# A planner that may put copies, roundings, lines and half of a weight's shift on either of two engines, and that reckons with instruction fetches

## The chip, the core and the metric

The kernel runs on one core of a Trainium2 chip. The metric is the device time of one execution in microseconds. The core has a matrix engine (PE), three engines for elementwise work (DVE, the vector engine; ACT, the scalar engine; POOL, GpSimd), and a queue on SP from which all loads and stores are issued to 16 DMA engines. Each engine takes its instructions strictly in order: an instruction that waits holds up all behind it on its engine.

## The reference

Attention over keys and values that are pooled eight to one, then a feed-forward layer whose activation is a rational function.

```python
k_p = k.reshape(B, H, Sp, pool, D).mean(axis=3)      # q, k, v: (8, 8, 576, 64), pool = 8
v_p = v.reshape(B, H, Sp, pool, D).mean(axis=3)
scores = scale * np.matmul(q, k_p.transpose(0, 1, 3, 2))
scores = scores - np.max(scores, axis=-1, keepdims=True)
attn = np.exp(scores)
attn = attn / (np.sum(attn, axis=-1, keepdims=True) + 1e-09)
x = np.matmul(attn, v_p)                              # as (4608, 512)
h = x @ w_in                                          # w_in: (512, 2048), w_out: (2048, 512)
P = a[0] + a[1] * h + a[2] * h2 + a[3] * h3           # h2 = h * h, h3 = h2 * h
Q = 1.0 + np.abs(b[0]) * np.abs(h) + np.abs(b[1]) * h2
out = (P / (Q + 1e-6)) @ w_out                        # the weights and a, b come as float64
```

## The kernel before

The 4608 tokens are 18 blocks of 256. The 2048 hidden columns are 8 units of 256, each with one slice of `w_in` and one of `w_out`. A step is one unit of one block in the first eight steps (blocks 0 and 1, units 0 to 3), later one half unit of two blocks. Its work is `mm1` (PE, into a PSUM bank `ph`), `rational` (tiles `w`, `r`, `rp`, `t`, then `gh` and `gl`, the rounded part and the rest) and `mm2` (PE, sums in two banks `po` of each block). Matrix products are made of float32 operands split in a rounded part and a rest, three products each. Blocks get their `x` by attention: `q` is loaded, turned by PE (`pq`) and copied by ACT (`qT`), PE makes `ps`, DVE, ACT and POOL the softmax `e`, PE turns that (`pm`, copies `am`) and makes `pv`, from which ACT and DVE split `x`. From block 4 on turning is done by DVE and small DMAs (`am<-e`, `am<-er`). The first eight steps, with four blocks of attention, eight weight slices and most large loads, fill the first 95 us or so; it is called the start here.

A float64 weight slice (`load_weights`) is turned to float32 thus: ACT makes `m` from the high words; for each half of the columns DVE shifts `m` left by three bits into a bank (`sh`) and joins to it the three top bits of the low word; ACT rounds the result into the weight and POOL makes the rest. In `quotient` (one rational), ACT makes `w` and `t` from `ph` and `r` from `w`, POOL multiplies `w` by `r`, DVE works on `t`, ACT makes `rp` (log, exp), DVE three more products, ACT rounds `gh`, and POOL makes `gl`.

The order on each engine is set by `Plan.solve`, a list scheduler that runs when the program is built. Every operation is tied to one engine, has a cost and a due time; the planner takes the operation that can start first, and among those within a window (`WIN`) the one of the lowest due time plus `SLOPE` times its delay. DMAs are costed by one bus that is free from `FIRST` on, and a landing time. `issue` writes the instructions out in that order (line 358 in the profile); where the plan leaves PE free while a `po` sum is open, it puts in small matmuls that add zeros to that sum, and before the first steps matmuls into a bank `idle` (line 349 both). They are called fillers here.

## Time and profile before

| | us |
|---|---|
| median of 3 runs (lowest to highest) | 871.18 (869.35 to 871.55) |
| the profiled execution | 871.99 |
| its span, from the first instruction to the last | 870.2 |
| PE busy | 853.6 (98%) |
| DVE busy | 684.1 (79%) |
| ACT busy | 637.6 (73%) |
| POOL busy | 566.1 (65%) |

The span is a little shorter than the execution's time; the rest lies around it. Fillers count as busy PE time. A group of instructions in the profile is named by output and inputs, without buffer numbers, so `gh<-t` is the rounding of all steps. In the timeline, the figure in brackets is how long the engine sat idle before the instruction and what ended that.

### The profile page before, as it was taken

The numbers are of one execution on the slowest core, as the hardware profiler recorded it, in microseconds if no ns is written. First come the engines' busy times: TensorE is split into PE (matmuls) and PEld (weight loads), VectorE is DVE, ScalarE is ACT, GpSimd is POOL, SyncE is SP. The second block draws the span as 40 slices with busy tenths as digits, with TensorE's granted clock in tenths as the row PEclk, the third lists the DMA queues.
The fourth block names the chain that finished last, engine by engine and source line by source line (L and its number), as shares of the span: only waits on it lengthen the run. The fifth ranks groups of instructions, "written<-read, shape, count | busy, mean of one in ns | idle before, by whom it ended". The sixth has DMA issues, their size and how long they took to land.

```text
span 870.2 us, 16357 instructions
## 1 busy us (share of the span) xinstructions
PE 853.6 (98%) x5628; PEld 745.9 (86%) x5628; DVE 684.1 (79%) x1155; ACT 637.6 (73%) x1098; POOL 566.1 (65%) x548
## 2 busy tenths in 40 slices
PE   8989999999999999999999999999999999999998
PEld 7779888898788888888888888878888888888897
DVE  5888998977877888868786878777877787876664
ACT  4889799875767776768777676868676777776764
POOL 4977788985767664677556765767666646464543
PEclk9999999999999999999999999999999999999999
DMA  9995621126244222224224422253124222020001
GB/s 323 324 336 171 193 48 49 32 57 171 62 95 92 74 34 51 42 71 92 68 32 89 99 40 54 65 106 67 38 43 102 38 54 32 30 35 27 25 1 50
DMA packets 191031, 74.23 MB, mean 85 GB/s; under 512 B 162276, under 2 KB 171876, under 8 KB 190948
## 3 DMA queue, kind: packets, MB, share of 16 engines
q1 hardware_dynamic: 190948, 73.18, 33.2%
q8 instruction: 45, 0.74, 0.4%
q14 instruction: 38, 0.31, 0.1%
HBM read 49.41 MB, written 12.58 MB: 71 GB/s over the span
## 4 chain that ended last, share of the span: by engine, by line
PE 81%; DMA 6%; SPq 4%; POOL 3%; issue 2%; ACT 2%; DVE 2%; POOLq 0%; DVEq 0%
PE po L358 37%; PE ph L358 37%; SPq L358 4%; DMA q<-in_q_dram 4%; PE pv L358 2%; PE ps L358 2%; POOL gl L358 1%; DVE t L358 1%; DMA early<-in_v_dram 1%; DMA st_k<-in_k_dram 1%; PE pm L358 1%; DMA st_r<-st_r 1%; PE po L349 1%; DMA ob<-pd 0%; POOL st_k L358 0%
## 5 line engine op out<-in xcount | busy, mean ns | idle before, releaser
L358 PE MATMUL ph<-x,win 128*128 128x512 f32 (+1 forms) x1920 | 428.1, 360 | 1.9 <-DVE t L358 0.7
L358 PEld LDWEIGHTS ph<-x,win 128*128 128x128 f32 x1920 | 337.2, 189 | 45.0 <-issue 2.1
L358 PE MATMUL po<-wout,gh 128*128 128x512 f32 x1152 | 288.9, 383 | 2.6 <-ACT gh L358 1.3
L358 POOL TENSOR_TENSOR w<-w,r 128x512 f32<-128x512 f32 (+1 forms) x145 | 184.8, 1275 | 115.6 <-ACT r L358 101.0
L358 POOL TENSOR_TENSOR gl<-t,gh 128x512 fp32r<-128x512 f32 (+1 forms) x145 | 184.4, 1273 | 95.5 <-ACT gh L358 87.3
L358 PEld LDWEIGHTS po<-wout,gh 128*128 128x128 f32 x1152 | 223.1, 198 | 26.6 <-ACT rp L358 1.5
L358 DVE SCALAR_TENSOR_TENSOR t<-t,abn,rp 128x512 f32<-128x512 f32 (+1 forms) x145 | 106.8, 737 | 98.1 <-ACT rp L358 97.4
L358 PE MATMUL po<-wout,gl 128*128 128x512 f32 x576 | 156.5, 381 | 0.0
L358 ACT ACTIVATE rp<-w 128x512 f32<-128x512 f32 (+1 forms) x145 | 86.9, 600 | 62.8 <-POOL w L358 53.4
L358 ACT ACTIVATE w<-ph 128x512 f32<-128x512 f32 (+1 forms) x145 | 85.9, 592 | 63.3 <-PE ph L358 59.2
L358 PEld LDWEIGHTS po<-wout,gl 128*128 128x128 f32 x576 | 112.4, 198 | 11.5
L358 ACT ACTIVATE t<-ph,abn 128x512 f32<-128x512 f32 (+1 forms) x145 | 111.1, 769 | 11.3 <-PE ph L358 11.1
L358 ACT ACTIVATE r<-w,abn 128x512 f32<-128x512 f32 (+1 forms) x145 | 116.9, 806 | 1.3 <-DVE rp L358 0.7
L358 DVE TENSOR_TENSOR t<-t,ph 128x512 f32<-128x512 f32 (+1 forms) x145 | 98.4, 678 | 22.7 <-ACT t L358 17.0
L358 DVE SCALAR_TENSOR_TENSOR t<-t,abn,ph 128x512 f32<-128x512 f32 (+1 forms) x145 | 106.6, 735 | 1.9 <-ACT w L358 0.2
L358 ACT CAST gh<-t 128x512 fp32r<-128x512 f32 (+1 forms) x145 | 88.8, 613 | 23.2 <-DVE t L358 21.2
L358 DVE SCALAR_TENSOR_TENSOR t<-rp,t 128x512 f32<-128x512 f32 (+1 forms) x145 | 98.3, 678 | 1.4
L358 DVE SCALAR_TENSOR_TENSOR rp<-w,rp 128x512 f32<-128x512 f32 (+1 forms) x145 | 99.0, 683 | 0.3
L358 ACT ACTIVATE rp<-rp 128x512 f32<-128x512 f32 (+1 forms) x145 | 84.8, 585 | 1.5
L358 POOL TENSOR_TENSOR e<-e,sm 128x576 f32<-128x576 f32 x36 | 40.9, 1151 | 7.6 <-DVE sm L358 6.3
L358 POOL TENSOR_TENSOR st_v<-st_v 128x512 f32<-128x512 f32 (+1 forms) x28 | 28.2, 1007 | 25.8 <-DMA st_v<-in_v_dram 24.6
L358 POOL TENSOR_TENSOR st_k<-st_k 128x512 f32<-128x512 f32 (+3 forms) x36 | 31.3, 868 | 19.3 <-DMA st_k<-in_k_dram 18.3
(99 smaller groups left out, 654.5 us busy)
## 6 DMA issues: line engine op xcount, KB each, us to landing
out_dram<-ob SPq DMA_DIRECT2D x17, 512.0 KB
rwin<-in_moe_w_in_dram SPq DMA_DIRECT2D x8, 1024.0 KB
rwout<-in_moe_w_out_dram SPq DMA_DIRECT2D x8, 1024.0 KB
st_v<-in_v_dram SPq DMA_DIRECT2D x28, 256.0 KB
am<-e SPq DMA_DIRECT2D x224, 32.0 KB
st_k<-in_k_dram SPq DMA_DIRECT2D x12, 512.0 KB
q<-in_q_dram SPq DMA_DIRECT2D x144, 32.0 KB
am<-er SPq DMA_DIRECT2D x224, 16.0 KB
```

The costliest lines, as they stand in the source:

```text
L349: self.nc.tensor.matmul(to, lhsT=self.filler, rhs=one, start=first, stop=first, skip_group_check=True)
L358: getattr(engines[op.eng], name)(*map(value, args), **{k: value(v) for k, v in kw.items()})
```

## The change

Operations can now have several ways, one per engine, each with its own cost (`Either`), and `solve` takes the engine on which such an operation can start first, after a handicap (`YIELD`) for the engine that is not its own. Copies and evictions (`copy`) may go to ACT or DVE, roundings (`cast`: `gh`, the weight, `kr`, `er`, `kpT`) to ACT or POOL, the line `t` to ACT or DVE, the line `r` to ACT or POOL. The left shift may be replaced: ACT then takes the top 16 bits of the low word and makes its three top bits by a scale and a rounding (bias `floor`), and DVE's joining instruction does the shift of `m` itself.

The planner also counts PE's instructions (two for each matmul and its weight load, four for those of unrounded float32), expects an instruction fetch at every 249 of them, and lets it delay DMAs that are under way by 1.15 us. Some costs and the windows have new values.

Over the whole program the order moves 84 of 143 full `r` and 47 of 143 `gh` from ACT to POOL, 35 of 143 full `t` from ACT to DVE, ten of 18 `ob` evictions on DVE to ACT, two `wout` and one `win` rounding and all seven `kr` to POOL; 15 of 32 shifts become an ACT instruction. In the start these are three `r`, five `gh` and one `wout` rounding on POOL, three `t` on DVE, and eight of the sixteen shifts of the first eight weight slices on ACT. Fillers: 50 into `idle` where 56 were; 48 into `po` in the first steps where 37 were, 39 of them in one place; and 7 later where one was.

```diff
@@ -151,13 +157,16 @@
     SURE = 20.0
 
     LOOK = 0.02
-    WIN = {"sp": 0.02, "pe": 0.02, "pool": 0.8, "dve": 0.02, "act": 0.3}
-    SLOPE = 20.0
+    WIN = {"sp": 0.02, "pe": 0.02, "pool": 0.3, "dve": 0.02, "act": 0.3}
+    SLOPE = 80.0
 
     SPARE, AFTER, SAFE = 0.0, 1.0, 0.0
 
     DEPTH = 128
-    FIRST, FLY, LAND = 3.1, 0.65, 0.6
+    FIRST, FLY, LAND = 2.35, 0.65, 0.6
+    FETCH, LONG, STEP = 249, 1.15, 0.108
+
+    YIELD = {"dve": 0.8, "act": 0.0, "pool": 0.0}
 
     MOVED = {}
 
...
@@ -237,8 +252,8 @@
             for e, cands in engs.items():
                 opts = found[e] = []
                 for op in cands:
-                    t = max(at[e], op.ready)
-                    if op.port:
+                    t = max(at[e], op.ready[e] + (self.YIELD[e] + op.shy if e != op.eng else 0.0))
+                    if op.ways[e][2]:
                         t = max(t, port)
                     if op.bytes:
                         t = max(t, landed[-8])
@@ -271,11 +286,14 @@
                 t, op = min(((t, op) for t, op in opts if t <= t0 + self.WIN[e]),
                             key=lambda x: (x[1].due + self.SLOPE * (x[0] - t0), x[1].seq))
                 if best is None or t < best[0]:
-                    best = t, op
+                    best = t, op, e
             assert best, "the plan is stuck at " + ", ".join(
                 str([b.name for b in op.bufs]) for c in engs.values() for op in c[:3])
-            t, op = best
-            engs[op.eng].remove(op)
+            t, op, e = best
+            for x in op.ways:
+                engs[x].remove(op)
+            op.eng = e
+            op.cost, op.calls, op.port = op.ways[e]
             for b in op.bufs:
                 if not b.held:
                     b.held = True
@@ -290,6 +308,19 @@
                 b.by[op.eng] = op.done
             if op.port:
                 port = op.end
+            if op.eng == "pe":
+                if t > at["pe"] and t < 100:
+                    steps += 2 * int((t - at["pe"]) / (0.215 if t < self.WARM else 0.12))
+                steps += op.steps
+                if steps >= goal:
+                    fetched = max(t, op.end - (steps - goal) * self.STEP / 2)
+                    goal += self.FETCH
+                    bus = max(bus, fetched) + self.LONG
+            if op.eng == "sp":
+                coming = max(at["pe"], t) + (goal - steps) * self.STEP
+                for x in (fetched, coming):
+                    if t < x + self.LONG and x < op.end:
+                        op.end = max(op.end, x + self.LONG + 0.4)
             if op.bytes:
                 begin = max(bus, op.end + self.FLY)
                 bus = begin + op.bytes
@@ -300,7 +331,9 @@
                 first, some, since, took = flow[oldest]
                 if issued - self.DEPTH > first:
                     op.end = max(op.end, since + took * (issued - self.DEPTH - first) / some)
-                op.done = bus + self.LAND + min(1.2, 0.4 * op.bytes) + (self.SAFE if bus > 100 else 0.0)
+                op.done = bus + self.LAND + min(0.4, 0.4 * op.bytes) + (self.SAFE if bus > 100 else 0.0)
+                if coming < op.done:
+                    op.done += self.LONG
                 landed.append(op.done)
             at[op.eng] = op.end
             for b in op.bufs:
...
@@ -372,6 +407,21 @@
                     self.eng, cost, [(name, args, kw)], port or self.eng == "pool", claims,
                     after=after)
         return Call()
+
+
+class Either:
+
+
+    def __init__(self, *ways):
+        self.ways = ways
+
+    def __call__(self, *args, claims=()):
+        (engine, n, name, extra), *others = self.ways
+        op = getattr(engine(n, claims=claims), name)(*args, **extra)
+        for engine, n, name, extra in others:
+            op.ways[engine.eng] = (engine.fixed + n * engine.rate / 1000, [(name, args, extra)],
+                                   engine.eng == "pool")
+        return op
 
 
 @with_exitstack
@@ -440,6 +490,17 @@
     dve = Engine(plan, "dve", 0.1, 1.04)
     act = Engine(plan, "act", 0.105, 0.85)
     gp = Engine(plan, "pool", 0.242, 2.021)
+    gp1 = Engine(plan, "pool", 0.2, 0.82)
+
+    def copy(n, first=act, scale=None):
+        ways = [(act, n, "copy", {}), (dve, n, "tensor_copy", {})]
+        if scale is not None:
+            ways = [(act, n, "activation", dict(func=AF.Copy, scale=scale)),
+                    (dve, n, "tensor_scalar", dict(scalar1=scale, scalar2=None, op0=ALU.mult))]
+        return Either(*ways) if first is act else Either(*ways[::-1])
+
+    def cast(n):
+        return Either((act, n, "copy", {}), (gp1, n, "tensor_copy", {}))
 
     def pe(ns, calls, claims=(), after=()):
         return plan.add("pe", ns / 1000, calls, claims=claims, after=after)
...
@@ -529,17 +592,23 @@
         hw, lw = words[:, :, 1], words[:, :, 0]
         m = new("dec", "m", [P, CW], F32, f"m_{name}")
         mi = m.bitcast(I32)
-        act(CW + 100).activation(m, hw.bitcast(F32), AF.Prelu, scale=2.0 ** -111, alpha=-2.0 ** 32)
+        act(CW + 250).activation(m, hw.bitcast(F32), AF.Prelu, scale=2.0 ** -111, alpha=-2.0 ** 32)
         for h in range(2):
             at = slice(h * CW // 2, (h + 1) * CW // 2)
             bits = bank(f"sh_{name}_{h}", [P, CW // 2]).bitcast(I32)
-            dve(CW // 2).tensor_scalar(
+            n = CW // 2
+            top = raw.bitcast(U16).rearrange("p (n t) -> p n t", t=4)[:, at, 1]
+            moved = dve(n).tensor_scalar(
                 out=bits, in0=mi[:, at], scalar1=3, scalar2=None, op0=ALU.logical_shift_left)
-            dve(CW // 2).scalar_tensor_tensor(
-                out=mi[:, at], in0=lw[:, at], scalar=29, in1=bits, op0=ALU.logical_shift_right,
-                op1=ALU.bitwise_or)
+            moved.ways["act"] = (act.fixed + (n + 130) * act.rate / 1000, [(
+                "activation", (bits, top, AF.Identity), dict(bias=floor, scale=2.0 ** -13))], False)
+            made = dict(out=mi[:, at], op1=ALU.bitwise_or, in1=bits)
+            low = dict(made, in0=lw[:, at], scalar=29, op0=ALU.logical_shift_right)
+            high = dict(made, in0=mi[:, at], scalar=3, op0=ALU.logical_shift_left)
+            both = dve(n).scalar_tensor_tensor(**low)
+            both.follow = moved, {"dve": both.calls, "act": [("scalar_tensor_tensor", (), high)]}
         w = new(kind, name, [P, 2, CW], F32R, name)
-        act(CW).copy(w[:, 0, :], m)
+        cast(CW)(w[:, 0, :], m)
         gp(CW).tensor_tensor(out=w[:, 1, :], in0=m, in1=w[:, 0, :].bitcast(F32),
                              op=ALU.subtract)
         weights[kind, u] = w
...
@@ -857,10 +922,7 @@
         pm = bank(name, [P, 4, P])[:SP]
         pe(110 * 4, [("transpose", (pm[:, x, :], row, ident), {}) for x, row in enumerate(rows)],
            claims=(am,))
-        if c == 0:
-            act(4 * P).copy(to, pm)
-        else:
-            dve(4 * P).tensor_copy(to, pm)
+        copy(4 * P, dve if c else act)(to, pm)
 
     def half(i, c, am, qs, es):
 
...
@@ -1088,8 +1150,12 @@
 
     def quotient(W, h, t, w, r, rp, gh, gl, early, late):
         act(W, claims=early).activation(w, h, AF.Abs, scale=1.0 / WS)
-        act(W + 200).activation(t, h, AF.Identity, bias=na2, scale=na3)
-        act(W + 260).activation(r, w, AF.Identity, bias=b0, scale=b1)
+        Either((act, W + 200, "activation", dict(func=AF.Identity, bias=na2, scale=na3)),
+               (dve, W + 100, "tensor_scalar", dict(scalar1=na3, scalar2=na2, op0=ALU.mult,
+                                              op1=ALU.add)))(t, h)
+        Either((act, W + 260, "activation", dict(func=AF.Identity, bias=b0, scale=b1)),
+               (gp1, W + 110, "tensor_scalar", dict(scalar1=b1, scalar2=b0, op0=ALU.mult,
+                                                   op1=ALU.add)))(r, w)
         gp(W).tensor_tensor(out=w, in0=w, in1=r, op=ALU.mult)
         dve(W).tensor_tensor(out=t, in0=t, in1=h, op=ALU.mult)
         dve(W + 50).scalar_tensor_tensor(
@@ -1102,7 +1168,7 @@
             out=rp, in0=w, scalar=QC, in1=rp, op0=ALU.add, op1=ALU.mult)
         dve(W).scalar_tensor_tensor(
             out=t, in0=rp, scalar=-2.0, in1=t, op0=ALU.add, op1=ALU.mult)
-        act(W, claims=late).copy(gh, t)
+        cast(W)(gh, t, claims=late)
         gp(W).tensor_tensor(out=gl, in0=t, in1=gh.bitcast(F32), op=ALU.subtract)
 
     pos, parts = {}, {}
@@ -1173,10 +1239,7 @@
 
     def evict(m, dst, po):
         dst, po = halves(dst), sorted_out(po)
-        if m == 0:
-            dve(DM).tensor_scalar(out=dst, in0=po, scalar1=1.0 / WS, scalar2=None, op0=ALU.mult)
-        else:
-            act(DM).activation(dst, po, AF.Copy, scale=1.0 / WS)
+        copy(DM, act if m else dve, 1.0 / WS)(dst, po)
 
 
     steps = [((i,), u, None) for i, u in
```

The order shows the move at three places. In the names the block or tile number stands behind the letters, then the unit; `pq6` turns the queries of tile 6, the first half of block 3.

**PE in the start**, where the sums of block 0 begin; `gh0_0` is the rounded rational of block 0 and unit 0. Before:

```order
L358 MATMUL ph0_3_839<-x_97,win3_796 128x256 x4
L358 MATMUL ph1_2_913<-x_97,win2_579 128x256 x16
L358 MATMUL po0_0_0_945<-wout0_693,gh0_0_747 128x512
L358 MATMUL po0_0_1_947<-wout0_693,gh0_0_747 128x512
L358 MATMUL pq6_950<-identr_95,q3_790 128x128 x4
L358 MATMUL po0_0_0_945<-wout0_693,gh0_0_747 128x512
```

And now:

```order
L393 MATMUL po0_0_0_939<-wout1_860,gl0_1_955 128x512
L393 MATMUL po0_0_1_941<-wout1_860,gl0_1_955 128x512
L393 MATMUL pq6_1036<-identr_95,q3_829 128x128 x4
L384 MATMUL po0_0_1_941<-zero_96,identr_95 128x256
L393 MATMUL ph1_3_1046<-x_97,win3_775 128x256 x24
L384 MATMUL po0_0_1_941<-zero_96,identr_95 128x256 x39
L393 MATMUL po0_0_0_939<-wout2_1041,gh0_2_1098 128x512
L393 MATMUL po0_0_1_941<-wout2_1041,gh0_2_1098 128x512
```

`pq6` stood behind the first two of block 0's `po` products; it now stands behind 24 of them (all of units 0 and 1), and eight more `ph1_2` products and four groups of `pm` stand ahead of it too. The wait for `gh0_2`, to which no filler led before, now has 39 ahead of it. On ACT the copy of `pq6` into `qT` moves with it from row 72 to row 84; on SP one of two stores of block 1's `x` (512 KB) has moved behind the load of `q3`.

**ACT in the first 20 us**, where the first two weights are made (`m_win0`, `m_win1`) and the softmax of block 0 is finished (`sm0`, `am0`). Before:

```order
L358 ACTIVATE sm0_0_282<-sm0_0_282,tiny_99 128x8
L358 COPY vp0_287<-pvs0_0_268 72x256
L358 ACTIVATE e0_238<-e0_238 128x576
L358 ACTIVATE m_win1_334<-rwin1_189 128x1024
L358 ACTIVATE sm0_1_301<-sm0_1_301,tiny_99 128x8
L358 COPY am0_0_347<-pm0_0_0_321 72x512
L358 COPY am0_0_347<-pm0_0_1_326 72x512
L358 CAST win0_356<-m_win0_279 128x1024
```

And now:

```order
L393 ACTIVATE sm0_0_277<-sm0_0_277,tiny_99 128x8
L393 ACTIVATE sh_win0_0_284<-rwin0_145,floor_100 128x512
L393 ACTIVATE sh_win0_1_287<-rwin0_145,floor_100 128x512
L393 ACTIVATE e0_234<-e0_234 128x576
L393 COPY vp0_295<-pvs0_0_264 72x256
L393 CAST win0_300<-m_win0_275 128x1024
L393 ACTIVATE sm0_1_297<-sm0_1_297,tiny_99 128x8
L393 COPY am0_0_344<-pm0_0_0_321 72x512
L393 COPY am0_0_344<-pm0_0_1_326 72x512
L393 ACTIVATE m_win1_348<-rwin1_185 128x1024
```

The second weight's first step stood ahead of the second sum `sm0_1` and both copies `am0_0`; now it stands behind them, and the two shifts and the rounding of the first weight stand ahead of them instead.

**POOL near the end of block 0's units 4 to 7**, some 205 us into the span before (`st_k3` are loaded keys of batch 3, `st_v2` loaded values of batch 2). Before:

```order
L358 TENSOR_TENSOR w0_6_2579<-w0_6_2579,r0_6_2591 128x512
L358 TENSOR_TENSOR gl0_5_2676<-t0_5_2471,gh0_5_2665 128x512
L358 TENSOR_TENSOR st_k3_0_2597<-st_k3_0_2597 128x2x256
L358 TENSOR_TENSOR w0_7_2626<-w0_7_2626,r0_7_2691 128x512
L358 TENSOR_TENSOR st_k3_0_2597<-st_k3_0_2597 128x2x128
L358 TENSOR_TENSOR ks3_0_2732<-st_k3_0_2597 128x256
L358 TENSOR_TENSOR gl0_6_2745<-t0_6_2550,gh0_6_2738 128x512
L358 TENSOR_TENSOR gl0_7_2789<-t0_7_2656,gh0_7_2778 128x512
```

And now:

```order
L393 TENSOR_TENSOR gl0_5_2605<-t0_5_2445,gh0_5_2579 128x512
L393 TENSOR_SCALAR r0_7_2625<-w0_7_2615,abn_449 128x512
L393 TENSOR_TENSOR st_v2_1_2572<-st_v2_1_2572 128x2x256
L393 TENSOR_TENSOR st_v2_1_2572<-st_v2_1_2572 128x2x128
L393 TENSOR_TENSOR vp0_295<-st_v2_1_2572 128x128
L393 TENSOR_TENSOR w0_7_2615<-w0_7_2615,r0_7_2625 128x512
L393 TENSOR_TENSOR gl0_6_2686<-t0_6_2519,gh0_6_2654 128x512
L393 TENSOR_TENSOR st_k3_0_2664<-st_k3_0_2664 128x2x256
L393 TENSOR_TENSOR gl0_7_2791<-t0_7_2621,gh0_7_2782 128x512
```

The first sum of `st_k3` stood ahead of `w0_7` and `gl0_6`; it now stands behind both, the sums of `st_v2_1` stand ahead of `w0_7` in its place, and `r0_7` is now POOL's too.

## Rows read from the trace of the kernel before

**Rows 1.** Windows view; columns: stretch, length, PE, PEld, DVE, ACT, POOL, clock, DMA, GB/s:

```profile
28.00:57.50 29.50, 28.25 (x341) 25.65 (x332) 28.90 (x59) 26.96 (x48) 27.73 (x25) 1.00 1.04 345
57.50:62.60 5.10, 1.73 (x9) 1.36 (x9) 4.99 (x9) 1.03 (x1) 3.40 (x3) 0.83 0.80 191
62.60:96.50 33.90, 33.90 (x321) 29.80 (x319) 28.41 (x51) 29.09 (x49) 24.61 (x21) 0.98 0.52 163
...
200.00:257.00 57.00, 54.01 (x349) 45.27 (x348) 45.15 (x78) 38.09 (x70) 40.37 (x42) 1.00 0.44 106
257.00:866.30 609.30, 608.11 (x3759) 530.42 (x3758) 469.71 (x783) 437.52 (x766) 369.73 (x353) 1.00 0.26 56
```

**Rows 2.** Timeline of PE (start, length, what; in brackets its idle before):

```profile
25.30 0.66 PE L358 MATMUL pq<-identr,q 128*128 128x128 f32 x4 [0.53 <-DMA q<-in_q_dram]
...
61.51 1.09 PE L358 MATMUL pq<-identr,q 128*128 128x128 f32 x4 [3.37 <-DMA q<-in_q_dram]
...
210.35 1.14 PE L358 MATMUL po<-wout,gh 128*128 128x512 f32 x4 [1.29 <-ACT gh L358]
...
227.55 1.06 PE L358 MATMUL po<-wout,gh 128*128 128x512 f32 x2 [1.16 <-DVE ob L358]
```

**Rows 3.** Windows view around 61 us, the same columns:

```profile
60.50:61.00 0.50, 0.00 (x0) 0.00 (x0) 0.50 (x2) 0.00 (x0) 0.40 (x1) 0.84 0.08 18
61.50:63.00 1.50, 1.49 (x6) 1.41 (x7) 0.99 (x2) 0.36 (x1) 0.00 (x0) 0.50 0.81 258
63.00:64.00 1.00, 1.00 (x4) 0.82 (x3) 0.00 (x0) 0.91 (x3) 0.00 (x0) 0.50 1.04 406
64.00:65.00 1.00, 1.00 (x5) 0.85 (x5) 0.05 (x1) 1.00 (x3) 0.00 (x0) 0.87 1.10 436
```

**Rows 4.** DMA view, 52.0 to 52.5 us: instruction queue (packets, MB, share):

```profile
q8 instruction: 1, 0.02, 12.3%
```

**Rows 5.** Timeline of ACT and DVE, first work after PE's wait:

```profile
62.64 0.58 ACT L358 COPY qT<-pq 128x512 f32<-128x512 f32 x1 [4.11 <-PE pq L358]
...
64.95 0.75 DVE L358 SCALAR_TENSOR_TENSOR t<-t,abn,rp 128x512 f32<-128x512 f32 x1 [2.46 <-ACT rp L358]
```

**Rows 6.** Timeline of ACT, of POOL, and the chain of work (115.75):

```profile
55.99 0.61 ACT L358 CAST gh<-t 128x512 fp32r<-128x512 f32 x1
...
58.52 1.28 POOL L358 TENSOR_TENSOR gl<-t,gh 128x512 fp32r<-128x512 f32 x1
...
115.75 1.73 PE po L358 x8
```

**Rows 7.** Timeline of PE, fillers in front of a pv product:

```profile
79.12 1.36 PE L349 MATMUL po<-zero,identr 128*128 128x256 f32 x10
```

**Rows 8.** Groups by shape, whole run (xcount | busy us, mean ns | idle before):

```profile
L358 POOL TENSOR_TENSOR w<-w,r 128x512 f32<-128x512 f32 x143 | 183.4, 1282 | 114.0 <-ACT r L358 99.4 <-DVE t L358 9.3 <-DMA q<-in_q_dram 3.5
...
L358 ACT ACTIVATE r<-w,abn 128x512 f32<-128x512 f32 x143 | 115.8, 809 | 1.3 <-DVE rp L358 0.7
...
L358 ACT CAST gh<-t 128x512 fp32r<-128x512 f32 x143 | 88.0, 616 | 21.2 <-DVE t L358 19.2 <-PE po L358 0.9 <-PE pk L358 0.4
...
L358 DVE TENSOR_SCALAR sh_win<-m_win 128x512 int32<-128x512 int32 x16 | 10.7, 694 | 3.7 <-ACT m_win L358 3.7
...
L358 ACT ACTIVATE m_win<-rwin 128x1024 f32<-128x1024 f32 x8 | 10.3, 1288 | 2.6 <-DMA rwin<-in_moe_w_in_dram 2.6
...
L358 POOL MEMSET pairs<- 128x208 f32 x1 | 0.3, 271 | 0.0
```

**Rows 9.** Timeline of ACT, the second weight's first step:

```profile
18.52 1.13 ACT L358 ACTIVATE m_win<-rwin 128x1024 f32<-128x1024 f32 x1 [2.62 <-DMA rwin<-in_moe_w_in_dram]
```

**Rows 10.** Timeline of POOL, and its waits (us, times, longest us):

```profile
206.03 1.27 POOL L358 TENSOR_TENSOR st_k<-st_k 128x512 f32<-128x512 f32 x1 [3.86 <-DMA st_k<-in_k_dram]
...
POOL st_v L358 <- DMA st_v<-in_v_dram: 24.6, 11, 5.9
...
POOL st_k L358 <- DMA st_k<-in_k_dram: 18.3, 10, 3.9
```

80 lines of the change are left out of this document (45 added, 35 removed).

## The prediction

> **What bounds the kernel now.** I read the page's busy times first. PE is busy for 853.6 of 870.2 us, so the other engines matter only where PE waits for them. The windows view then says where that is. From 257 us to PE's end PE is busy for 608.11 of 609.30 us; in the start and in the passage from 200 to 257 us, where it has 54.01 of 57, it is not [rows 1]. From 28 to 57.5 us DVE is busy for 28.90 of 29.50 us, more than any other engine: there it is the fullest. The timeline of PE names the waits: 3.37 us for a `q` load at 61.51, 0.53 us for another at 25.30, 1.29 us for `gh` at 210.35 and 1.16 us for `ob` at 227.55 [rows 2]. Two losses hide in the busy time: fillers, and 61.5 to 65 us, where the granted clock is 0.50 and then 0.87 behind the long wait [rows 3]. Of PE's two levels, 1.2 and 2.4 GHz, 0.50 is the lower.
>
> The long wait is the reader's main exhibit. PE stands in front of `pq`, behind it in order the `po` products. ACT has the copy of `pq` next and idles 4.11 us, DVE behind ACT 2.46 us [rows 5]. One late load stops three engines. While PE waits the DMA engines move 18 GB/s at a busy share of 0.08 [rows 3], about one engine of 16: all but one have brought their part. Eight us earlier an instruction fetch took 12.3% of 16 engines for 0.5 us [rows 4], that is 0.125 x 16 x 0.5 = 1.0 us of one engine. That the late engine is the one with the fetch is a reading; the rows don't name engines.
>
> The page "Runtime: NRT & Kernel Launch" of the Trainium skill (Instruction fetch mechanics) speaks against reckoning with fetches: the sequencer streams its code by itself, and the cost of crossing a block is mostly hidden. It holds for the engine that fetches; the row shows 1.0 us that the loads beside it don't get. By that rule the first rival below would have no chance; by the row it keeps its own.
>
> **The change, part by part.** The sum is made against the profiled execution, 871.99 us with a span of 870.2, and carried over to the median, 871.18, which is 0.8 lower.
>
> *The wait at 61.51.* `pq6` now has 22 more `po` products ahead of it. Eight take 1.73 us [rows 6], 0.216 each, so 22 take 4.8 us; eight `ph` products and four groups of `pm` come on top and aren't counted. PE came to the wait at 61.51 - 3.37 = 58.14, and would now come at 62.9 or later; the load had landed by 61.5. Cover of 1.4 us, and one store of 512 KB has left its front. Do the products' inputs hide it? `gh` of unit 1 ended at 55.99 + 0.61 = 56.60 and `gl` at 58.52 + 1.28 = 59.80 [rows 6], while the first `gl0_1` product comes 16 products, 3.5 us, after 57.5, at 61.0. They do. ACT's copy now stands 12 rows later, at 0.6 us or more each 7 us, against its 4.11 us of idling. The 3.37 us go, and with them the slow clock: half of 2.5 us and 0.13 of 1 us, 1.38. **-4.75**; ends -4.75 and, if the load is late again, -1.4.
>
> *Fillers.* Ten take 1.36 us [rows 7], 0.136 each. In the first steps 11 more: **+1.5**. Next late after the removed wait is `gh0_2`, and the 39 fillers there, 5.3 us, stand whether it is ready or not; so PE can't come out ahead of them. Six more later: +0.8, counted with the passage. Six fewer in `idle` are put at 0, since loads end the waits there.
>
> *Engines in the start.* Eight shifts leave DVE at 0.694 us [rows 8], -5.6; three `t` come at about the same price, +2.1; net -3.5 of the 28.9 us in which it is full. ACT gets eight shifts at half the price of a 1024-column step from the same raw weight, 1.288 / 2 = 0.64, +5.2, and loses three `r` (0.809) and five `gh` (0.616), -5.5: even. POOL gets eight of these and a `wout` rounding. The trace has no copy or line on POOL. Its nearest rows are a memset of 208 columns, 0.271 us, and a two-input product of 512 columns, 1.282 us [rows 8]. I take the memset scaled to 512 columns, 0.67, as one input is nearer to none than to two loops of the same; ends 0.27 and 1.28. That makes 8 x 0.67 + 1.33 = 6.7 us, and POOL has 33.90 - 24.61 = 9.3 us free from 62.6 to 96.5 [rows 1]: covered; at 1.28 it is 12.6 and isn't. PE loses 29.50 - 28.25 = 1.25 us from 28 to 57.5, of which a freer DVE can give back 0 to 1.25: **-0.6**.
>
> The page "GPSIMD Engine Reference" of the Trainium skill (When to use GPSIMD, Engine selection) speaks against POOL for elementwise work, but says that one-input work runs roughly at line rate; its 1.03 cycles an element at 1.2 GHz give an estimate of 0.44 us and a start-up for 512 columns. No row here shows it. By that the third rival has less chance than by rows alone.
>
> *First 28 us.* ACT's wait of 2.62 us for a weight load at 18.52 [rows 9] no longer stands ahead of `sm0_1` and `am0_0`; but two shifts and a rounding do, which wait for DVE. What PE gains is mostly lost again in front of the `q` load at 25.30 [rows 2], except for products done meanwhile: eight `ph` of half a `po`'s columns, 0.9 us. **-0.4**, ends -0.9 and +0.5.
>
> *The passage from 200 to 257 us.* POOL waited 3.86 us for `st_k` [rows 10] with `w` and `gl` behind it, and PE's 1.29 us at 210.35 followed. Both now stand ahead of that load: -1.3. In its place stand sums of `st_v2`, a load issued earlier. The 1.16 us for `ob` wait on a load and stay. With the six fillers **-0.5**; ends -2.2 (all 2.99 us lost there go, fillers stay) and +1.3 (POOL is caught by the other load).
>
> *From 257 us on.* PE waits 1.19 us in all. ACT, DVE and POOL have room: POOL gets 131 operations, 88 us at 0.67, on 566.1, and comes to 654 of 870 (75%); at 1.28 to 734 (84%). **0**, ends -1.2 and the third rival.
>
> Sum: -4.75 + 1.5 - 0.6 - 0.4 - 0.5 = -4.75; 871.99 becomes 867.2, and the median 871.18 becomes 866.4.
>
> **The rivals.** *The load is late again.* The plan's moments for fetches differ from the chip's, and a fetch or the stores meet `q3` anew; cover is 1.4 us. ACT then holds `rp0_2` behind the copy, DVE the next step of `t`, and `gh0_2` comes after its 39 fillers. For it speaks that a single engine's lateness cost over 1 us [rows 3]; against it, the extra work ahead. The first term keeps its 1.38 only: 866.4 + 3.4 = 869.8.
>
> *All waits go.* Fuller use of DVE and ACT and later `st_k` sums clear what can be cleared: lower ends throughout, -4.75 + 1.5 - 1.25 - 0.9 - 2.2 - 1.2 = -8.8, 862.4. Against it: the fillers show that waits remain in the plan.
>
> *POOL becomes the bound, and the kernel slower.* One-input work costs 1.28 us. From the first moved `r` of block 1 on, six such operations follow on POOL in the start; each is 0.61 longer, 3.7 us in front of `gh` and `gl`, if POOL has no slack. Later it is 84% busy, and its waits for loads, 11 for `st_v` and 10 for `st_k` [rows 10], of which I can follow one to PE, are not made up: four more that cost 1.29 us each are 5.2. 866.4 + 8.9 = 875.3. It decides from some 1.0 us an operation on (half of that excess takes the gain). For it: POOL's own rows are slow; against it: it waits 114.0 us in front of `w` alone [rows 8], so it has slack in most steps.
>
> **How the numbers follow.** The forecast, 864 to 868.5, has 0.58; all waits go 0.15; the load late again 0.17; POOL the bound 0.10. About 0.3%, 2.6 us, is what a measurement of this kernel can tell from no change, so faster means under 868.6 and slower over 873.8. Forecast and clear-out make 0.73, less 0.04 for the forecast's upper edge: faster 0.69. Late load and that edge make 0.21, and 0.01 of POOL's case: same 0.22. Slower 0.09. The range runs from 862.0, the clear-out, to 871.0, past the late load; POOL's case and the tails, some 0.15, are outside.
>
> **What would show it.** Right: no wait over 0.5 us on PE and a granted clock of 1.00 from 50 to 70 us; a block of 39 fillers with little idle time behind it; one-input POOL rows near 0.67 us; the wait at 210 gone; the passage's PE loss nearer to 1.5 than to 3 us. Wrong: PE idle behind the fillers at `gh0_2` by more than 2 us; a `q` load that ends a wait over 2 us in the start; POOL one-input rows over 1.0 us; more than 3 us of PE idle after 257 us, which would mean that the new order is worse where I put 0.

## The result, and the profile after

| | median, us | lowest to highest | runs |
|---|---|---|---|
| before | 870.26 | 868.57 to 871.55 | 4 |
| changed | 858.58 | 858.41 to 858.70 | 4 |

The ratio is 0.9867 (95% interval 0.9847 to 0.9887): 11.7 us faster, where 4.8 were forecast. The time lies below the range (862.0), and so below the 862.4 of the rival in which all waits go.

The page of the changed kernel, busy times:

```profile
PE 848.6 (99%) x5639; PEld 744.5 (87%) x5639; DVE 690.1 (81%) x1155; ACT 549.0 (64%) x954; POOL 662.2 (77%) x693
```

Windows view, the stretches of [rows 1] (columns as there):

```profile
28.00:57.50 29.50, 29.42 (x359) 27.42 (x351) 28.45 (x56) 27.91 (x49) 29.36 (x26) 1.00 1.07 344
57.50:62.60 5.10, 5.10 (x34) 4.53 (x33) 4.55 (x9) 5.03 (x8) 5.10 (x6) 1.00 0.95 273
62.60:96.50 33.90, 33.90 (x289) 29.49 (x288) 28.56 (x52) 28.13 (x45) 30.11 (x26) 1.00 0.60 194
...
200.00:257.00 57.00, 57.00 (x357) 49.51 (x350) 45.39 (x76) 34.76 (x65) 47.55 (x53) 1.00 0.39 92
257.00:853.00 596.00, 596.00 (x3710) 520.84 (x3708) 476.48 (x789) 350.11 (x627) 441.73 (x464) 1.00 0.26 55
```

From 28 us to its end PE has 0.08 us of gaps. Waits view of PE, all that it lists; every one lies before 27 us:

```profile
PE idle L393 <- DVE identr L1316: 1.8, 1, 1.8
PE pk L393 <- DVE early L393: 0.9, 2, 0.7
PE pm L393 <- POOL e L393: 0.8, 1, 0.8
PE pq L393 <- DMA q<-in_q_dram: 0.7, 2, 0.5
```

ACT fell from 637.6 to 549.0 us and POOL rose from 566.1 to 662.2. The groups by shape of what was moved, and of the product `w` behind POOL's `r` (columns as in [rows 8]):

```profile
L393 POOL TENSOR_TENSOR w<-w,r 128x512 f32<-128x512 f32 x143 | 183.5, 1283 | 15.6 <-ACT r L393 11.3
...
L393 POOL TENSOR_SCALAR r<-w,abn 128x512 f32<-128x512 f32 x84 | 64.9, 773 | 75.2 <-ACT w L393 71.6 <-DMA q<-in_q_dram 1.0 <-PE po L393 0.8
...
L393 POOL CAST gh<-t 128x512 fp32r<-128x512 f32 x47 | 28.8, 613 | 13.0 <-DVE t L393 11.6 <-PE ph L393 0.9 <-POOL ks L393 0.2
```

```profile
L393 ACT ACTIVATE sh_win<-rwin,floor 128x512 int32<-128x512 uint16 x8 | 6.5, 844 | 0.0
```

```profile
L393 DVE TENSOR_SCALAR t<-ph,abn 128x512 f32<-128x512 f32 x35 | 28.1, 804 | 14.4 <-ACT w L393 11.8 <-POOL st_r L393 1.4 <-POOL gh L393 0.8
```

POOL makes an `r` in 0.773 us and a `gh` in 0.613; DVE's `t` takes 0.804 and ACT's shift 0.844. ACT's shift takes longer than the one on DVE that it replaces (0.694 [rows 8]). POOL's wait in front of `w` went from 114.0 us [rows 8] to 15.6, but 75.2 us now stand in front of the `r` that it makes itself.

**A measure for all that follows.** Idle time understates what PE loses. A wait costs some 0.2 to 0.3 us more than its gap until products follow each other at full pace again: in the kernel before, by the measure below, the gap of 0.66 us in front of the `ph` at 30.34 costs 0.89, and the 1.29 us at 210.35 cost 1.62. This is called a restart here. And a fall of the clock hides in busy time. So I summed every trace thus. The distance from each matmul's start to the next start, less the median distance for its shape and tile over all traces, is loss, and so is the time up to PE's first instruction; a filler counts with its whole distance, and apart. The products alone come to 792.7 us in every trace, and products, fillers and loss make PE's end.

| us | products | fillers | other loss | PE's end |
|---|---|---|---|---|
| before, first trace | 792.7 | 16.6 | 57.4 | 866.7 |
| before, second trace (e9) | 792.7 | 16.0 | 55.8 | 864.5 |
| changed, first trace | 792.7 | 16.7 | 43.7 | 853.1 |
| changed, second trace (e13) | 792.7 | 16.8 | 44.3 | 853.9 |

Each row is one execution, the profiled one. Most of the loss seems to belong to the program (changes of shape, runs of small products): no kernel here came below 43.7. So the fillers cost in sum what they cost before, and the whole gain is loss that went: waits, the restarts behind them and slow clock.

The long wait, in the timeline of PE of the changed kernel and, of POOL, the `gh0_2` for which the 39 fillers stand:

```profile
62.30 0.60 PE L393 MATMUL pq<-identr,q 128*128 128x128 f32 x4
...
65.53 4.53 PE L384 MATMUL po<-zero,identr 128*128 128x256 f32 x39
69.90 0.60 PE L393 MATMUL po<-wout,gh 128*128 128x512 f32 x2
```

```profile
68.13 0.61 POOL L393 CAST gh<-t 128x512 fp32r<-128x512 f32 x1
```

`pq6` comes at 62.30 with no wait, and the clock of 1.00 stays. `gh0_2` is done at 68.74; its first product starts 1.16 us after that, behind the fillers.

### The profile page after: what moved, and what is told of

It reads as the page before. It is cut to its first block, busy times and chain, and to the rows that moved or that the text cites. A ratio compares the mean times of both kernels' runs of the same rounds, so it can differ in the third digit from the quotient of the medians.

```text
span 856.6 us, 16346 instructions
## 1 busy us (share of the span) xinstructions
PE 848.6 (99%) x5639; PEld 744.5 (87%) x5639; DVE 690.1 (81%) x1155; ACT 549.0 (64%) x954; POOL 662.2 (77%) x693
## 4 chain that ended last, share of the span: by engine, by line
PE 97%; DMA 2%; ACT 0%; SPq 0%; DVE 0%; issue 0%
PE po L393 44%; PE ph L393 44%; PE pv L393 3%; PE ps L393 3%; DMA q<-in_q_dram 1%; PE po L384 1%; DMA early<-in_k_dram 1%; PE pm L393 1%; PE pk L393 1%; PE pq L393 0%; SPq L393 0%; PE pvs L393 0%; DVE early L393 0%; PE pl L393 0%; PE pw L393 0%; ACT kpT L393 0%
## 5 line engine op out<-in xcount | busy, mean ns | idle before, releaser
L393 PE MATMUL ph<-x,win 128*128 128x512 f32 (+1 forms) x1920 | 418.8, 360 | 0.0
L393 POOL TENSOR_TENSOR w<-w,r 128x512 f32<-128x512 f32 (+1 forms) x145 | 185.0, 1276 | 15.6 <-ACT r L393 11.3
L393 POOL TENSOR_SCALAR r<-w,abn 128x512 f32<-128x512 f32 (+1 forms) x85 | 65.5, 770 | 75.8 <-ACT w L393 72.2
L393 ACT ACTIVATE t<-ph,abn 128x512 f32<-128x512 f32 (+1 forms) x109 | 84.1, 773 | 26.6 <-PE ph L393 24.2
L393 ACT CAST gh<-t 128x512 fp32r<-128x512 f32 (+1 forms) x98 | 59.9, 612 | 36.8 <-DVE t L393 34.4
L393 ACT ACTIVATE r<-w,abn 128x512 f32<-128x512 f32 (+1 forms) x60 | 48.4, 807 | 1.3 <-POOL w L393 0.3
L393 DVE TENSOR_SCALAR t<-ph,abn 128x512 f32<-128x512 f32 (+1 forms) x36 | 28.7, 797 | 15.5 <-ACT w L393 12.8
```

The source lines that it names most:

```text
L393: getattr(engines[op.eng], name)(*map(value, args), **{k: value(v) for k, v in kw.items()})
```

## The experiments

Each time stands against runs of the kernel before on the same chip; loss and fillers are those of the one execution that was profiled. Theory A was that the choice of engine makes the gain, theory B that the planner's truer numbers do, fetches among them; the rival to both, that a few waits were moved by a lucky order.

**Either half alone.** e1 holds every operation to its own engine:

```diff
         for op in self.ops:
+            op.ways = {op.eng: op.ways[op.eng]}
             later, hold, op.shy = self.MOVED.get(op.seq, (0.0, 0.0, 0.0))
```

> The changed kernel with every operation held to its own engine; the new planner numbers and the reckoning with fetches stay. If the choice of engine makes the gain (theory A), this is back at 867 to 872 us and PE waits in the start as before. If the better numbers make it (theory B: a plan that the chip follows), it keeps most of the gain, 858 to 862 us, and shows no wait of PE over 1 us after 28 us. If both are needed in part, 863 to 866 us.

Measured 871.97 us (before 869.26; ratio 1.0031, 1.0019 to 1.0043). e2 keeps the ways and gives the planner its old numbers back (the old costs of `m` and of the small softmax steps too, left out below):

```diff
-    WIN = {..., "pool": 0.3, ...}; SLOPE = 80.0; FIRST = 2.35; FETCH = 249
+    WIN = {..., "pool": 0.8, ...}; SLOPE = 20.0; FIRST = 3.1; FETCH = 10 ** 9
-                op.done = bus + self.LAND + min(0.4, 0.4 * op.bytes) + ...
+                op.done = bus + self.LAND + min(1.2, 0.4 * op.bytes) + ...
```

> The changed kernel with all its ways, but with the planner's numbers of before (windows, slope, first load, landing, the costs of m and of the small softmax steps) and without the reckoning with fetches. Theory A (engines) expects 858 to 862 us. Theory B (numbers) expects 866 to 871 us and a wait of PE for a load of q or of a weight of more than 2 us in the start, which the plan didn't foresee.

Measured 872.83 us (1.0039, 1.0026 to 1.0052). Neither half is worth anything alone, which neither theory had foreseen, but they fail in different ways. e1 waits for no load after 28 us; its loss is 46.5 us, near the changed kernel's, and it has 27.6 us of fillers, as its group shows (the changed kernel has x55, 7.2 us busy). e2 has 17.8 us of fillers and 58.4 of loss, with a wait for a `q` load in the timeline of PE. The group of e1, then the wait of e2:

```profile
L385 PE MATMUL po<-zero,identr 128*128 128x256 f32 x136 | 20.2, 281 | 0.0
```

```profile
25.77 0.63 PE L393 MATMUL pq<-identr,q 128*128 128x128 f32 x4 [2.72 <-DMA q<-in_q_dram]
```

So the numbers turn waits that the plan didn't see into gaps that it sees and fills. That the ways close such gaps is what the changed kernel's 16.7 us of fillers suggest; e11 and e10, below, show how much of that is the order's.

**The reckoning with fetches.** e3 takes out that alone:

```diff
-    FETCH, LONG, STEP = 249, 1.15, 0.108
+    FETCH, LONG, STEP = 10 ** 9, 1.15, 0.108
```

> The changed kernel with only the reckoning with fetches taken out (one expected at the 10 to the 9th instruction). If the fetches are what made loads late for the plan (the reading behind the first term of the prediction), a wait of PE for a load of 1 to 4 us comes back in the start and the time is 860 to 864 us. If the order alone moved the wait away, it stays within 1 us of the changed kernel, 858 to 859.6 us.

Measured 869.28 us (0.9999, 0.9986 to 1.0012), loss 53.7: the whole gain is gone, more than I had allowed for. The execution in the trace is the fastest of twelve, 867.49 us, with the clock at 1.00 throughout, so the clock isn't what it lost. By the measure above it loses 3.4 us more than the changed kernel up to 114 us, 1.3 from there to 195, 2.7 in the passage from 195 to 264 us and 1.5 behind it: the reckoning matters along the whole program, and not at the first loads alone.

Do fetches come as the plan says? The DMA view of the changed kernel has, for the instruction queue of [rows 4] (packets, MB, share):

```profile
q8 instruction: 45, 0.74, 0.4%
```

The page counts 5639 products and as many weight loads on PE, so there is one such packet for each 251 instructions; the plan says 249. In the trace a packet takes 0.88 to 1.51 us, 1.13 in the mean; the plan says 1.15. From one packet to the next PE starts between 118 and 370 instructions. So the plan has the number and the length of fetches right, and the single moment only roughly.

Was e3 an unlucky order? e12 is a second order without fetches (`SLOPE` 90 beside the edit of e3), and e11 another order with them:

```diff
-    SLOPE = 80.0
+    SLOPE = 60.0
```

> The changed kernel without the reckoning with fetches and with the slope at 90, so a second order that was planned without fetches, beside that of e3. If the reckoning is what keeps PE from unforeseen waits, the loss outside fillers is 51 to 58 us, as in e2, e3 and e7, with a wait of over 1 us for a q load, and the time is 865 to 872 us. If e3 was an unlucky order, the loss is 43 to 47 us and the time 857 to 861 us.

> The changed kernel with the planner's slope at 60 in place of 80; every way and the reckoning with fetches stay. The order comes out otherwise from the start on, and the planner puts more fillers in. If the reckoning makes the waits foreseen, the loss outside fillers stays within 43 to 47 us while fillers rise, and the time is 864 to 870 us by fillers alone. If slope has no part in it, 858 to 860 us.

e12: 873.35 us (1.0038, 1.0019 to 1.0057), loss 60.3, fillers 16.0. e11: 866.99 us (0.9971, 0.9959 to 0.9983), loss 43.9, fillers 24.9. e11 came as expected; e12 came out worse than the ranges named, on the side of the reckoning. In every plan that reckons with fetches in full, and whose fillers stand, the loss is 44 to 47 us; in the four without it (e2, e3, e7, e12) it is 54 to 60.

But e11 has every way and the reckoning, and still 24.9 us of fillers, near the 27.6 of e1. On its chip it is worth 3.1 us (870.09 before), where the slope of 80 gives 11.7 and e10, below, 13.1. So the drop in loss is shown in several orders, and how much of it reaches the time hangs on the order that the slope picks. Other slopes were not tried in the kernel before.

e7 asks whether any caution does it, every load being taken to land 1.15 us later, and no fetches:

```diff
-                op.done = bus + self.LAND + min(0.4, 0.4 * op.bytes) + ...
+                op.done = bus + self.LAND + 1.15 + min(0.4, 0.4 * op.bytes) + ...
```

> The changed kernel without the reckoning with fetches, but with every load expected 1.15 us later than it was. If any caution about loads does the same (theory: pessimism), 858 to 861 us and no wait for a q load over 1 us. If it matters which loads are taken to be late (theory: the fetches), 863 to 870 us, either with waits or with more fillers than the 16.7 us of the changed kernel.

874.26 us (1.0058, 1.0043 to 1.0073), loss 56.5, slower than either expectation: caution about each load isn't enough. One place where the orders differ is the first `q` load. It lands at much the same moment everywhere; here are the first transposes of it in the timelines of PE of the changed kernel, e3, e7 and e12:

```profile
25.22 0.63 PE L393 MATMUL pq<-identr,q 128*128 128x128 f32 x4 [0.46 <-DMA q<-in_q_dram]
```

```profile
25.09 0.41 PE L393 MATMUL pq<-identr,q 128*128 128x128 f32 x2 [1.84 <-DMA q<-in_q_dram]
```

```profile
25.74 0.48 PE L393 MATMUL pq<-identr,q 128*128 128x128 f32 x1 [2.35 <-DMA q<-in_q_dram]
```

```profile
25.29 0.88 PE L393 MATMUL pq<-identr,q 128*128 128x128 f32 x4 [1.92 <-DMA q<-in_q_dram]
```

In all it ends between 25.1 and 25.8 us. The changed kernel has four more `ph` products than e12 and eight of `pv` in front of it, and waits 0.46 us; the others come to it 1.8 to 2.4 us early. And the wait isn't all: behind it e2, e7 and e12 run at the lower of PE's two levels for some ten us (windows view of e12); e3 does not. Nor is it the longest: e7 and e12 wait 3.74 and 3.99 us for DVE at 114 and 113 us, in front of `ph` (the last line is e12's), and the clock falls once more there.

```profile
25.00:26.00 1.00, 0.71 (x5) 0.74 (x6) 0.00 (x0) 0.00 (x0) 1.00 (x2) 0.76 1.01 393
26.00:34.00 8.00, 8.00 (x89) 6.00 (x88) 4.40 (x12) 5.00 (x8) 7.58 (x8) 0.50 1.04 384
34.00:36.00 2.00, 2.00 (x12) 2.00 (x12) 2.00 (x6) 1.05 (x3) 0.61 (x1) 0.56 1.14 325
```

```profile
113.09 1.10 PE L393 MATMUL ph<-x,win 128*128 128x512 f32 x4 [3.99 <-DVE t L393]
```

Two more runs split the reckoning. e15 keeps only that a fetch takes bus time, e16 only that it holds SP's issue and the loads under way:

```diff
 e15
-                    if t < x + self.LONG and x < op.end:
-                        op.end = max(op.end, x + self.LONG + 0.4)
-                if coming < op.done:
-                    op.done += self.LONG
 e16
-                    bus = max(bus, fetched) + self.LONG
```

> The changed kernel with half of the reckoning: a fetch still takes 1.15 us from the bus, but neither SP's issue nor a load that is under way is held by itself. If the bus time is what matters, the loss outside fillers stays at 43 to 47 us and no q load is waited for by over 1 us; the time is then that of the fillers, 858 to 863 us. If not, 53 to 60 us of loss and 866 to 873 us.

> The changed kernel with the other half of the reckoning: SP's issue and loads near a fetch are held by themselves, and the bus loses nothing to it. If holding the loads is what matters, the loss outside fillers stays at 43 to 47 us and the time is 861 to 866 us by its fillers; if the bus time is, 53 to 60 us of loss, a wait for a q load of over 1 us, and 866 to 873 us.

e15: 865.39 us (0.9963, 0.9942 to 0.9983), loss 50.3. e16: 866.55 us (0.9969, 0.9955 to 0.9983), loss 48.0, fillers 19.8. Either loss lies between the two that were expected, and each still waits over 1 us for a `q` load (1.68 and 1.13); so either half does a part, by one order each. A bus that is slower by the same amount all the time, with no moments of fetches, was not tried: whether the moments matter, or only the amount, is open.

**Which ways, and where.** e5 takes away the ways to POOL, e6 all ways of operations that are due after 110 us:

```diff
 e5
+            if op.eng != "pool":
+                op.ways.pop("pool", None)
 e6
+            if op.due > 110:
+                op.ways = {op.eng: op.ways[op.eng]}
```

> The changed kernel without the ways to POOL: r, gh and the weights' roundings stay on ACT; copies, the lines t and the shifts may still go to ACT or DVE; the new numbers and the reckoning with fetches stay. If POOL's share is what pays (theory P: 131 operations off the two fuller engines), the time is 866 to 872 us, most of the lost time being fillers and not waits, as in the run with own engines. If it is the exchange between ACT and DVE that pays, 858 to 862 us.

> The changed kernel in which an operation may change its engine only if its due time is up to 110 us; later ones keep their own. The gain by progress was 7.5 us up to 115 us and 6 us after. If the ways work in the start alone and the passage's gain came from the order, 858 to 860 us; if the ways are what clears the passage and what follows, the start stays as in the changed kernel and 5 to 6 us are lost later, 863 to 866 us.

e5: 866.85 us (0.9970, 0.9957 to 0.9983), loss 44.9, fillers 24.0. e6: 863.96 us (0.9941, 0.9924 to 0.9958), loss 44.0, fillers 21.6. Without POOL two thirds of the 11 us of fillers between e1 and the changed kernel stay. By trace e6 ends 5.1 us later than the changed kernel: 0.4 of it lies before 28 us, 4.0 in the passage, with 4.4 us of fillers there against 0.9, and 0.7 behind it. So in this order the passage's gain needs the ways, and what comes after it hardly does. The sums of either run are no price of the ways by themselves, as e11 with every way has as many fillers (24.9 us). Their filler groups:

```profile
L386 PE MATMUL po<-zero,identr 128*128 128x256 f32 x110 | 16.8, 282 | 0.0
```

```profile
L386 PE MATMUL po<-zero,identr 128*128 128x256 f32 x97 | 12.6, 276 | 0.0
```

**Two moves by hand in the kernel before** (e4): `pq6` and its copy behind 20 more `po` products, the sums of `st_k3` behind `w0_7` and `gl0_6`. Below, `p` and `c` are the turning and its copy, `pe[last]` is the first `pm4` product, `behind` is ACT's `t0_3`, `late` are the sums, `pool[last]` is `gl0_6`.

```diff
-        self.order = order
+        self.order = by_hand(order)
...
+    order.remove(p)
+    order.remove(c)
+    order.insert(order.index(pe[last]), p)
+    order.insert(max(order.index(behind), order.index(p)) + 1, c)
...
+    at = order.index(pool[last]) + 1
+    order[at:at] = late
```

> The kernel before with two moves by hand and nothing else: pq6 and its copy of the queries stand 20 po products later, and the sums of st_k3 on POOL stand behind w0_7 and gl0_6. The prediction's terms say that the first gives 4.75 us (3.37 of waiting and 1.38 of slow clock) and the second 1.3, so 864.2 us against 870.3. The rival, that the waits come back at the next late input (gh0_2 in the start), gives 867 to 870 us.

865.32 us (0.9957, 0.9944 to 0.9970): 3.9 of the 6.05, between the two expectations. The first move gave all that was there. PE comes to `pq6` at 62.08 without a wait:

```profile
62.08 0.60 PE L358 MATMUL pq<-identr,q 128*128 128x128 f32 x4
```

The second took the 1.29 us at `gh` away, and 1.9 us (against the first trace of before) or 2.5 (against e9) were given back ten us later. PE now waits 1.54 us in front of `ob`, only 0.4 more than the 1.16 before [rows 2]. The larger part is the clock: behind this wait PE runs at 0.50 for 3.4 us, about half of which is lost, where in the kernel before it stays at 1.00 (windows view of e4, then of before). At the end of the passage the move is worth some 0.7:

```profile
221.42 1.12 PE L358 MATMUL po<-wout,gh 128*128 128x512 f32 x2 [1.54 <-DVE ob L358]
```

```profile
222.30:225.70 3.40, 3.40 (x10) 2.75 (x9) 3.32 (x8) 2.36 (x6) 0.89 (x3) 0.50 0.32 72
```

```profile
227.50:231.00 3.50, 3.32 (x15) 2.60 (x16) 3.47 (x7) 2.27 (x6) 1.48 (x2) 1.00 0.31 63
```

e9 is the kernel before again, for a second trace.

> The kernel before, once more, for a second trace of it. If its waits are a matter of the order alone, PE waits for the load of q ahead of pq6 by 3.0 to 3.7 us again, the ratio is 1.00 and no stretch differs by over 0.5 us from the first trace. If loads land at other moments from run to run, that wait differs by more than 1 us, and with it the time within 867 to 872 us.

870.30 us (1.0001, 0.9982 to 1.0019). The wait at `pq6` is 0.5 us shorter, which neither expectation had, and the clock behind it is not the same (timeline of PE and windows view of e9):

```profile
60.92 0.63 PE L358 MATMUL pq<-identr,q 128*128 128x128 f32 x4 [2.88 <-DMA q<-in_q_dram]
```

```profile
61.50:63.00 1.50, 1.50 (x9) 1.37 (x8) 1.11 (x2) 1.32 (x3) 0.00 (x0) 1.00 0.96 370
63.00:64.00 1.00, 1.00 (x7) 0.90 (x6) 0.09 (x1) 1.00 (x3) 0.00 (x0) 1.00 1.10 420
64.00:65.00 1.00, 1.00 (x6) 0.93 (x5) 0.66 (x1) 1.00 (x2) 0.52 (x1) 1.00 1.05 422
```

At this place the first trace of before is 1.9 us dearer (3.37 us of wait and the slow clock of [rows 3], against 2.88 and none); everywhere else the two agree within 0.8 us.

**The fillers** (e8: the 48 in open `po` sums of the start left out):

```diff
-                elif sums:
+                elif sums and free is not None and op.start > 110:
```

> The changed kernel without the 48 fillers that stand in open po sums in the start (39 of them ahead of gh0_2); nothing else. In the trace of the changed kernel POOL ends the cast of gh0_2 at 68.74 us and the first product of it starts at 69.90, so the fillers overrun by some 1.1 us. If they are only cover, PE waits some 3.3 us there and the time falls by 0.5 to 1.2 us, to 857.4 to 858.1. If a pause of that length lowers the granted clock behind it, as behind the wait of 3.37 us before (1.38 us lost), it comes out at 858.5 to 860 us.

861.52 us (0.9910, 0.9881 to 0.9938), against 858.58 (0.9867): 2.9 us slower, beyond both expectations; 2.6 between the traces. PE waits 3.15 us at `gh0_2`, starts its products 1.05 us earlier, and loses that and 0.9 us more at the lower clock (timeline of PE, windows view):

```profile
68.85 0.85 PE L393 MATMUL po<-wout,gh 128*128 128x512 f32 x2 [3.15 <-POOL gh L393]
```

```profile
68.50:70.00 1.50, 1.15 (x4) 0.60 (x4) 1.50 (x3) 1.46 (x3) 1.42 (x2) 0.76 1.07 415
70.00:71.00 1.00, 0.97 (x29) 0.85 (x30) 1.00 (x3) 0.87 (x1) 1.00 (x3) 0.50 1.00 401
71.00:72.00 1.00, 1.00 (x16) 0.77 (x9) 0.93 (x3) 0.85 (x2) 1.00 (x2) 0.50 0.54 213
72.00:73.00 1.00, 1.00 (x7) 0.80 (x6) 1.00 (x3) 0.00 (x0) 1.00 (x2) 0.65 0.00 0
```

The eight fillers at 74.67, left out too, make up for that: the next product starts at 75.65 in e8 and at 75.66 in the changed kernel. What is lost for good comes later, first in a wait that the changed kernel doesn't have (timeline of PE of e8). Why DVE is later there stays open.

```profile
83.47 0.60 PE L393 MATMUL pm<-identr,e 128*72 128x128 f32 x4 [1.30 <-DVE t L393]
```

So leaving the fillers out gains nothing around `gh0_2`, and they are cover there; not all of the 2.9 us is the clock.

**A faster order.** e10 and e14 change the pace by which the first eight steps come due:

```diff
-    HEAD, SLOW, ... = 15.5, 5, ...
+    HEAD, SLOW, ... = 15.5, 5.5, ...
```

> The changed kernel with one number changed, the pace by which the first eight steps come due, 5.5 in place of 5; every way and the reckoning with fetches stay. The plan that follows has other fillers and waits. If PE's loss outside fillers is what the reckoning holds down (43.7 us in the changed kernel, 44 to 46.4 in the three runs that kept the reckoning), it stays within 43 to 47 us, and the time follows the fillers alone: 855 to 859 us by 1 to 3 us fewer of them in the start. If the changed kernel was one fortunate order, waits come back and it is 861 us or more.

> The changed kernel once more. If its order no longer hangs on the moment at which a load lands, its runs stay within 1 us of each other around 858.6 and its trace repeats the first one, with the loss outside fillers at 43 to 45 us; if it was fortunate in its first runs, they scatter over 3 us or more, as those of the kernel before do (867.0 to 873.8).

> The changed kernel with the first eight steps coming due at a pace of 5.5 in place of 5, on the same chip as e13. By e10 it is 1.6 us faster than the changed kernel (856.5 to 858.1 us); if that was the chip's doing, both come out within 0.5 us of each other.

e10: 857.02 us (0.9852, 0.9834 to 0.9870), fillers 12.0, loss 46.3: 4.7 us of fillers went and 2.6 of loss came, so the time doesn't follow the fillers alone. On one chip, e13 (the changed kernel again) has 859.20 (858.61 to 860.14, five runs, so 1.5 us apart where 1 was expected) and e14 857.52 (856.97 to 858.59, four runs). The runs don't overlap, if barely: some 1.7 us, and it beats both kernels. It has 12 fillers in `po` where the changed kernel has 55.

## Why the prediction was wrong

The direction was right and the size was not: more than half of the gain was missed. Three steps failed. In the passage I said that the wait for `ob` stays; from 257 us on I put 0; and the reckoning with fetches, which in the runs keeps the loss some 10 us lower, had no term in the sum. The terms for the first 57 us and for the fillers were mis-sized. By the measure above, at the same places in PE's work (changed kernel's first trace against both traces of before):

| part of PE's work | forecast | against first trace | against e9 |
|---|---|---|---|
| start, up to `pq6` | -1.0 | -3.2 | -3.1 |
| the wait at 61.51 and the clock behind it | -4.75 | -4.8 | -2.9 |
| from there to 114 us, fillers | +1.5 | +0.5 | +0.5 |
| 114 to 195 us | 0 | +0.5 | +0.5 |
| the passage, 195 to 264 us | -0.5 | -4.2 | -4.3 |
| the rest | 0 | -2.4 | -2.1 |
| sum | -4.75 | -13.6 | -11.4 |

- **The long wait, right.** It went, and the slow clock with it. `pq6` comes at 62.30, a little earlier than the 62.9 that was forecast, as PE had gained 3 us ahead of it. Only its size was one execution's: in e9 the same order costs 1.9 less. I carried the sum over to the median by 0.8 for everything; this one term should have had -2.9 beside -4.75.
- **Engines in the start and the first 28 us, mis-sized.** I said that what PE gains before the `q` load at 25.30 is lost again in front of it, "except for products done meanwhile", and then took 0.4. It has done twelve `ph` products there and not four, and waits 0.46 us instead of 0.53. The 1.25 us of gaps from 28 to 57.5 us went down to 0.08. Both lower ends, together 2.15, were passed by 1 us, some of it restarts: the two gaps over 0.3 us before, 1.18 us at 30.34 and 50.83, cost 1.65 by the measure above. ACT's shift cost 0.844 us where 0.64 was taken, and DVE's `t` 0.804 where 0.7 was; neither made PE wait.
- **Fillers, mis-sized.** The count was right (39 in a block), and the price came out at 0.116 us each in that block, not 0.136. So the 48 of now cost 5.5 us where the 37 before cost 5.2: 0.3 us more and not 1.5. I also took them as cost alone, and they are cover: `gh0_2` isn't ready before 68.74, so at most 1.2 of the block's 4.5 us are lost, and e8, without them, is not faster.
- **The passage, the failed step.** "The 1.16 us for `ob` wait on a load and stay". e4 shows that this holds, and that the gain at `gh` is given back there, if only POOL's order changes. e6 shows that the passage's gain needs the ways: without them there, 4.0 us of it are lost, 3.5 of these to fillers. And the plan moved SP's issue as well, the queue that I hadn't followed to this place. Timelines of SP and DVE, of before and of the changed kernel:

```profile
212.13 8.78 SPq L358 DMA_DIRECT2D q<-in_q_dram  x18
221.02 2.00 SPq L358 DMA_DIRECT2D am<-e  x3
223.07 0.60 SPq L358 DMA_DIRECT2D ob<-pd  x1
```

```profile
226.71 1.29 DVE L358 SCALAR_TENSOR_TENSOR ob<-po,ob 128x512 f32<-128x512 f32 x2 [0.73 <-DMA ob<-pd]
```

```profile
208.20 1.42 SPq L393 DMA_DIRECT2D q<-in_q_dram  x3
209.79 1.26 SPq L393 DMA_DIRECT2D am<-e  x2
211.15 1.23 SPq L393 DMA_DIRECT2D am<-er  x2
212.43 0.59 SPq L393 DMA_DIRECT2D ob<-pd  x1
```

```profile
216.32 1.29 DVE L393 SCALAR_TENSOR_TENSOR ob<-po,ob 128x512 f32<-128x512 f32 x2
```

  `ob`'s load stood behind 18 `q` pieces in a row and three `am`; now it stands behind three and four, and DVE doesn't wait for it. That the new place is the cause is read from these rows; no run moves this load alone. All 2.99 us of idle time went, and some 2 us of restarts and other loss, against 0.9 us of new fillers.
- **From 257 us on, the failed step.** I put 0 against 1.19 us of idle time. All of it went, with its restarts. e6, with no ways there, keeps most of that (0.7 us lost), so the order and the numbers do the larger part.
- **POOL the bound, fallen.** Its operations cost 0.773 and 0.613 us, about the 0.67 taken and far from 1.28; POOL is busy for 662 us (654 worked out). The estimate by the page "GPSIMD Engine Reference" of the Trainium skill (its cycles an element stand in Elementwise — side-by-side cycle accounting), 0.44 us and a start-up, is not far under the cast's 0.613; the line with two operations takes 0.773.
- **Fetches, the failed step.** I treated them as a rival (the load late again) and not as a part of the change with a price, so the sum has nothing for them. By e3 and e12 the reckoning is what lets the ways pay: 10.7 us and more between these and the changed kernel; e15 and e16 keep a part of it. The page "Runtime: NRT & Kernel Launch" of the Trainium skill (Instruction fetch mechanics) says that the cost of crossing a block is mostly hidden; taken for the loads beside a fetch too, that would make the reckoning worth nothing, and the runs speak against it. That a fetch holds one engine's share of the loads remains a reading: no row names engines.
- **The signs named ahead.** No wait of PE and a clock of 1.00 from 50 to 70 us, POOL's rows near 0.67, the wait at 210 gone, a block of 39 fillers with no gap behind it: all came. The passage's idle time went to 0 and not to 1.5 us.
- **Chances.** "All waits go" had 0.15 and 862.4. It was the case that came, and its price was low by the restarts and other loss that goes with a wait, and by the fillers. The forecast took the list of waits one by one and asked of each whether the moved rows beside it clear it. But the change made the whole plan anew with better numbers, so each wait had a common reason to go. The size is in part luck of the order: at another slope (e11) the same change is worth 3.1 us, which is under the 4.8 forecast.

## What to carry to other kernels

A planner's freedom pays only as far as its plan comes true on the chip: here freedom without the right delays gave nothing (e2, e3), and right delays without freedom turned waits into fillers (e1). Split PE's time into products, planned gaps and unplanned loss; the first says what is left, the second how good the order is, the third how true the plan is. One order is one sample: the same planner gave 857, 858.6 and 867 us with one number changed. A wait costs more than its gap, and a queue of DMA issues that a new plan reorders has to be followed to every wait in the sum.

## What the runs showed of the hardware

- How long a wait is doesn't say alone whether the clock falls. Behind 3.37 us [rows 3], 3.15 us (e8) and 1.54 us (e4) PE ran at 0.50 for some 2.8, 3.4 and 3.4 us, and behind 1.92 us in e12 for ten; behind 2.88 us in e9 and 1.84 us in e3 it stayed at 1.00. What PE did ahead of the wait differs too; the cause was not tried.
- PE's instruction queue brought one packet of 16 KB for each 251 of its instructions, of 1.13 us in the mean (45 packets in the changed kernel).
- POOL's one-input work on 512 columns takes five to six tenths of the time of its two-input products (0.613 and 0.773 us against 1.283).
- On one chip the kernel before scatters by 5.9 us (867.26 to 873.17, 21 runs beside e13), e15 by 7.2 (ten runs), and the changed kernel by 1.5 (858.61 to 860.14, five runs). In e15 the five executions with a mean clock of 0.999 to 1.000 take 863.4 to 864.4 us, and the five with 0.993 to 0.996 take 866.4 to 870.5: there the scatter goes with the clock.
